# Top-k attention with mixture of depths: the 32nd greatest score from a bound, an exact count and one MAX8, with the exponential moved behind the transposes

## The chip, the core and the metric

The program runs on one core of one Trainium2 chip. The time is device time in microseconds (us) of one execution of the whole program. PE is the matmul engine, PEld its weight loads, DVE the vector engine, ACT the scalar engine, POOL the GpSimd engine, SP the engine that issues most DMAs.

## The reference

```python
def _attn_ref(q, k, v):                       # q, k, v: 8 batches, 8 heads, 576 tokens, 64 wide, f32
    scores = scale * np.matmul(q, k.transpose(0, 1, 3, 2))        # scale = 1 / 8
    kth = np.partition(scores, -32, axis=-1)[..., -32:-31]
    scores = np.where(scores >= kth, scores, -1000000000.0)
    attn = np.exp(scores - np.max(scores, axis=-1, keepdims=True))
    attn = attn / (np.sum(attn, axis=-1, keepdims=True) + 1e-09)
    return np.matmul(attn, v)

def _moe_ref(x, w_gate, w1, w2, capacity):    # x: 8 batches, 576 tokens, 512 wide; capacity = 128
    scores = np.einsum('bsd,d->bs', x, w_gate)
    out = x.copy()
    for b in range(B):
        top_idx = np.argpartition(-scores[b], capacity)[:capacity]
        ye = np.maximum(x[b, top_idx] @ w1, 0.0) @ w2             # 512 -> 1024 -> 512
        g = 1.0 / (1.0 + np.exp(-scores[b, top_idx]))
        out[b, top_idx] = x[b, top_idx] + g[:, None] * ye
```

The attention output, heads side by side, is the `x` of the second part. Everything is f32.

## The kernel before

Work is cut into 160 **units**: 8 batches, in each 5 tiles of queries, for each tile 4 pairs of heads. Four of the five query tiles have 128 tokens; there a unit makes two **score tiles** of 128 rows by 576 keys, one for each head of the pair (128 such units, "two-tile units"). The last query tile has 64 tokens, and both heads share one score tile (32 "one-tile units"). That makes 288 score tiles.

All four compute engines run their instructions strictly in the order in which the main loop writes them (the class `InOrder`, whose line 33 stands on nearly every row of the profile), so an instruction that waits holds back all that is written behind it on its engine. The loop is a software pipeline over units. In the turn of unit n:

- PE multiplies the scores of unit n + 1 (`scores`, tile `ps`), then the product with v of unit n - 2 (`values`, tile `small`: 10 matmuls, 20 in the trace, since each f32 product is two), then transposes the weights of unit n - 1 (`turn`, tiles `ptr` and `small`).
- DVE finds each row's 32nd greatest score of unit n (`top_k`): four times MAX8 (the 8 greatest of a row), between them three times MATCH_REPLACE8, which overwrites the 8 just found. The two tiles of a unit alternate.
- ACT copies scores out of PSUM (`sc`), copies the transposed weights out of PSUM (`pT`), copies the result of `values` (`xs`), and makes the exponential `e`.
- POOL, in `weigh`, makes `shift` (minus the greatest score), the mask `p` (score at or above the 32nd), and the product of `p` and `e`.

The **mixture** of a batch (ranks by gate score, gathering of 128 tokens as a matmul with a one-hot matrix `pick`, two dense layers) is a generator whose steps go one to a unit behind the unit's own work, in the first ten units of the next batch. On PE its steps are `xe_ps`, `extra_ps`, twice `h_ps`, `y_ps`. The **loads** of the next batch's q, k and v go one step to a unit in the units 11 to 18 of a batch: each asks SP for rows and transposes rows fetched earlier (`tr`, on PE, with copies to `kT` or `qT` on ACT). The kernel ends with the mixture of the last batch, beside nothing.

Of the kernel before, what the change touches and what calls it, by code (L numbers as in the profile page):

```python
# [15 lines left out]
# Below every score: what match_replace puts in place of the values already taken.  # L16
# [3 lines left out]
# Full tiles of 128 tokens; token 4 * p + j sits on partition p of tile j, so that  # L20
# a partition's four tokens are contiguous in memory. The last 64 tokens are tile J.
# [3 lines left out]
class InOrder:  # L25
    """An engine whose instructions stay in the order in which they are written."""
# [10 lines left out]
def kernel(  # L37
# [29 lines left out]
    ldpool = ctx.enter_context(tc.tile_pool(name="ld", bufs=2))  # L67
    kqpool = ctx.enter_context(tc.tile_pool(name="kq", bufs=2))
    scpool = ctx.enter_context(tc.tile_pool(name="sc", bufs=6))
    wkpool = ctx.enter_context(tc.tile_pool(name="wk", bufs=4))  # L70
    stats = ctx.enter_context(tc.tile_pool(name="stats", bufs=12))
    ppool = ctx.enter_context(tc.tile_pool(name="p", bufs=3))
    ptpool = ctx.enter_context(tc.tile_pool(name="pt", bufs=4))
# [11 lines left out]
    # The place of each token in its sequence, and the row of slots 0 .. CAP-1.  # L85
# [8 lines left out]
    # before[p, t, c] = 1 where the token of column c comes before token (p, t):  # L94
    # of tokens with the same gate score, the earlier one is taken first.
# [24 lines left out]
    # v with a column of ones: the product with it is the softmax's denominator.  # L120
# [28 lines left out]
    def load_qkv(b, qT, kT, vt):  # L149
        """In 2 * NHP steps, k and q of a pair of heads; each asks for the next one's rows."""  # L150

        def fetch(src, hp, name):
            rows = ldpool.tile([P, NT, 2, D], FP32, name=name)
            for hh in range(2):
                nc.sync.dma_start(
                    out=rows[:, 0:J, hh, :],
                    in_=src[b, 2 * hp + hh, 0:JP, :].rearrange("(p j) d -> p j d", j=J),
                )
            nc.sync.dma_start(
                out=rows[0:R, J, :, :],  # L160
                in_=src[b, 2 * hp : 2 * hp + 2, JP:S, :].rearrange("h p d -> p h d"),
            )
            return rows
# [4 lines left out]
            for src, dst, name in ((k, kT, "kin"), (q, qT, "qin"))  # L168
        ]
        fetched = {}  # L170
        for i, (src, dst, hp, name) in enumerate(todo):
# [5 lines left out]
            for c in range(J):  # L177
# [15 lines left out]
                in_=v[b, i, 0:JP, :].rearrange("(p j) d -> p j d", j=J),  # L193
            )
            nc.sync.dma_start(out=vt[0:R, i, J, 0:D], in_=v[b, i, JP:S, :])
            yield

    def top_k(scs):
        """Of each tile's rows, the greatest score and the least of the TOP_K greatest."""
        cur, left, first = list(scs), {}, {}  # L200
        for r in range(TOP_K // 8):
            best = {}
            for i in range(len(scs)):
                best[i] = stats.tile([P, 8], FP32, name="best" if r else "first")
                dve.max(best[i], cur[i])
            first = first or best
            if r < TOP_K // 8 - 1:
                for i in range(len(scs)):
                    if r == 0:
                        left[i] = wkpool.tile([P, S], FP32, name="left")  # L210
                    dve.match_replace(left[i], best[i], cur[i], LOWEST)
                    cur[i] = left[i]
        return [(first[i][:, 0:1], best[i][:, 7:8]) for i in range(len(scs))]
# [9 lines left out]
    def scores(t, hp, qT, kT):  # L223
        """The pair's score tiles; two heads' products go to banks of their own."""
# [11 lines left out]
        scs = []  # L236
        for ps in pss:
            sc = scpool.tile([P, S], FP32, name="sc")
            act.copy(
                out=sc.rearrange("p (u s) -> p u s", u=2), in_=ps[:, :, 0:HALF]  # L240
            )
            scs.append(sc)
        return scs

    def weigh(scs, tops):
        """exp(scale * (score - greatest)) where a score is among its row's TOP_K, else 0."""
        weights = []
        for sc, (top, kth) in zip(scs, tops):
            shift = stats.tile([P, 1], FP32, name="shift")
            pool.tensor_scalar_mul(shift, top, -scale)  # L250
            e = ppool.tile([P, S], FP32, name="e")
            act.activation(e, sc, AF.Exp, bias=shift, scale=scale)
            p = ppool.tile([P, S], FP32, name="p")
            pool.tensor_scalar(
                out=p, in0=sc, scalar1=kth, scalar2=None, op0=ALU.is_ge
            )
            pool.tensor_tensor(p, p, e, ALU.mult)
            weights.append(p)
        return weights

    def turn(weights):
        """The weights transposed, [key, chunk of keys, query]."""
        small = ps_small.tile([P, 512], FP32, name="small")
        turned = []
        for i, p in enumerate(weights):
            pT = ptpool.tile([P, NT, P], FP32, name="pT")
            tr = ps_tr.tile([P, 512], FP32, name="ptr")
            for c in range(J):
                pe.transpose(
                    tr[:, c * P : (c + 1) * P], p[:, c * P : (c + 1) * P], ident  # L270
                )
            pe.transpose(small[0:R, i * P : (i + 1) * P], p[:, JP:S], ident)
            act.copy(
                out=pT[:, 0:J, :], in_=tr.rearrange("p (c i) -> p c i", c=J)
            )
            act.copy(out=pT[0:R, J, :], in_=small[0:R, i * P : (i + 1) * P])
            turned.append(pT)
        return turned, small

    def values(t, hp, turned, small, vt, xs):  # L280
        """The weights' product with v, and their sums, into the heads' columns of xs."""
        n = R if t == J else P
        for pT, heads in zip(turned, heads_of(t)):
            for hh, r in heads:
                for c in range(NT):
# [3 lines left out]
                        pT[0:rows, c, r : r + n],  # L289
# [9 lines left out]
    def normalise(n, xs, x):  # L299
        den = stats.tile([P, H], FP32, name="den")  # L300
# [11 lines left out]
    def route(gate, rank):  # L312
        """Each token's rank by gate score, [token, tile]."""
# [15 lines left out]
        for t in range(NT):  # L329
# [3 lines left out]
            tied = modpool.tile([P, S], FP32, name="tied", tag="scratch", bufs=2)  # L333
# [18 lines left out]
    def mixture(b, x, gate):  # L352
        """In steps, that go between those of the next batch's attention."""
# [3 lines left out]
        # What goes with a token to its slot: its row of out, and sigmoid(gate).  # L357
# [3 lines left out]
        for t0, t1, n in ((0, J, P), (J, NT, R)):  # L361
            dve.tensor_scalar_add(
                out=extra[0:n, t0:t1, 0], in0=tok_i[0:n, t0:t1], scalar1=float(b * S)
            )
            # exp(88) is finite, and its reciprocal below the least normal number.
# [71 lines left out]
        gy = modpool.tile([P, HD], FP32, name="gy", bufs=2)  # L437
        act.activation(gy, ps, AF.Copy, scale=g)
        # Every token has its x in out by then; a slot's token gets g * y on top.
# [8 lines left out]
    def gates(t, x, gate):  # L448
        n = R if t == J else P
        prod = modpool.tile([P, S], FP32, name="prod", tag="scratch", bufs=2)  # L450
# [11 lines left out]
    def store(b, x):  # L462
        nc.sync.dma_start(
            out=out[b, 0:JP, :].rearrange("(p j) n -> p j n", j=J), in_=x[:, 0:J, :]
        )
        nc.sync.dma_start(out=out[b, JP:S, :], in_=x[0:R, J, :])
# [8 lines left out]
    load_from = per_batch - 1 - 2 * NHP  # L475
# [6 lines left out]
    for n in range(-1, len(units) + 3):  # L482
# [3 lines left out]
        if n + 1 < len(units):  # L486
            b, t, hp = units[n + 1]
            made[n + 1] = scores(t, hp, *qkv[b][0:2])
# [71 lines left out]
```

## Time and profile before

| | |
|---|---|
| median of 3 runs | 1803.62 us (1800.26 to 1804.66) |
| span of the profiled execution | 1801.2 us |
| DVE busy | 1552.2 us (86%) |
| PE busy, weight loads busy | 1432.4 us (80%), 1114.2 us (62%) |
| POOL busy | 1052.5 us (58%) |
| ACT busy | 687.1 us (38%) |
| chain that ended last | DVE 42%, PE 27%, POOL 15%, issue 13%, ACT 3% |

The profiled execution has no other time of its own than its span. The span lies 2.4 us below the median of the runs, and inside their scatter. Busy time is an average over stages; the chain (followed back from the last instruction to what released each) is spread over three engines, so which engine sets the pace has to be read stage by stage. The granted clock of PE has two levels in this trace, 0.50 (1.2 GHz) and 1.00 (2.4 GHz).

### The profile page before, as it was taken

The numbers are of one execution on the slowest core, as the hardware profiler recorded it, in microseconds if no ns is written. First come the engines' busy times: TensorE is split into PE (matmuls) and PEld (weight loads), VectorE is DVE, ScalarE is ACT, GpSimd is POOL, SyncE is SP. The second block draws the span as 40 slices with busy tenths as digits, with TensorE's granted clock in tenths as the row PEclk, the third lists the DMA queues.
The fourth block names the chain that finished last, engine by engine and source line by source line (L and its number), as shares of the span: only waits on it lengthen the run. The fifth ranks groups of instructions, "written<-read, shape, count | busy, mean of one in ns | idle before, by whom it ended". The sixth has DMA issues, their size and how long they took to land.

```text
span 1801.2 us, 22598 instructions
## 1 busy us (share of the span) xinstructions
PE 1432.4 (80%) x7320; PEld 1114.2 (62%) x7320; DVE 1552.2 (86%) x3281; ACT 687.1 (38%) x1505; POOL 1052.5 (58%) x931
## 2 busy tenths in 40 slices
PE   5888777897778977789778897688876988769875
PEld 3667556575566756667557675576655866557554
DVE  7999798888988889887998879987799878998872
ACT  3444433344333443334433344333443334433330
POOL 5767465565656655556655566555665556655660
PEclk8766666857567575776757766577665767658767
DMA  7101200012000120001200112001120011000000
GB/s 196 35 5 29 70 3 1 13 27 73 1 1 13 27 73 1 0 13 29 71 1 1 19 28 66 1 1 20 30 63 1 1 19 37 4 1 1 7 24 9
DMA packets 120486, 45.77 MB, mean 25 GB/s; under 512 B 116144, under 2 KB 116144, under 8 KB 119344
## 3 DMA queue, kind: packets, MB, share of 16 engines
q1 hardware_dynamic: 119216, 42.23, 9.2%
q0 software_dynamic: 1152, 2.10, 0.9%
q8 instruction: 58, 0.95, 0.2%
q14 instruction: 60, 0.49, 0.1%
HBM read 32.77 MB, written 11.53 MB: 25 GB/s over the span
## 4 chain that ended last, share of the span: by engine, by line
DVE 42%; PE 27%; POOL 15%; issue 13%; ACT 3%; DMA 0%; POOLq 0%; SPq 0%; ACTq 0%; DVEq 0%
DVE left L33 15%; DVE best L33 15%; POOL p L33 13%; PE small L33 11%; DVE first L33 5%; PE ptr L33 4%; PE ps L33 4%; DVE tied L33 4%; PE h_ps L33 3%; PE tr L33 2%; PE xe_ps L33 1%; POOL shift L33 1%; DVE prod L33 1%; POOL x L33 1%; ACT e L33 1%
## 5 line engine op out<-in xcount | busy, mean ns | idle before, releaser
L33 POOL TENSOR_SCALAR p<-sc,best 128x576 f32<-128x576 f32 x288 | 526.0, 1827 | 211.3 <-DVE best L33 159.5
L33 DVE MAX8 best<-left 128x8 f32<-128x576 f32 x864 | 613.8, 746 | 4.4
L33 PEld LDWEIGHTS small<-v,pT 128*128 128x128 f32 (+3 forms) x3200 | 510.3, 237 | 138.5 <-issue 71.0
L33 PE MATMUL small<-v,pT 128*128 128x65 f32 (+3 forms) x3200 | 579.3, 336 | 2.1 <-ACT pT L33 2.1
L33 POOL TENSOR_TENSOR p<-p,e 128x576 f32<-128x576 f32 x288 | 407.2, 1414 | 282.7 <-ACT e L33 266.3
L33 PE MATMUL ptr<-ident,p 128*128 128x128 f32 x1152 | 279.1, 387 | 284.6 <-POOL p L33 284.5
L33 DVE MATCH_REPLACE8 left<-best,left 128x576 f32<-128x576 f32 x576 | 423.2, 741 | 0.0
L33 PEld LDWEIGHTS ptr<-ident,p 128*128 128x128 f32 x1152 | 187.7, 195 | 333.2 <-POOL p L33 320.1
L33 ACT ACTIVATE e<-sc,shift 128x576 f32<-128x576 f32 x288 | 223.4, 776 | 412.9 <-POOL shift L33 412.7
L33 PE MATMUL ps<-kT,qT 64*128 64x288 f32 (+1 forms) x1280 | 294.8, 583 | 1.1 <-ACT qT L33 1.1
L33 DVE MAX8 first<-sc 128x8 f32<-128x576 f32 x288 | 202.8, 740 | 75.0 <-ACT sc L33 74.9
L33 ACT COPY pT<-ptr 128x512 f32<-128x512 f32 x288 | 170.2, 591 | 221.6 <-PE ptr L33 221.4
L33 DVE MATCH_REPLACE8 left<-first,sc 128x576 f32<-128x576 f32 x288 | 211.6, 741 | 0.0
L33 PEld LDWEIGHTS ps<-kT,qT 64*128 64x128 f32 (+1 forms) x1280 | 159.7, 250 | 58.9 <-issue 16.1
L33 ACT COPY sc<-ps 128x576 f32<-128x576 f32 x288 | 169.0, 631 | 19.0 <-PE ps L33 18.0
L33 POOL TENSOR_TENSOR x<-xs,rden 128x512 f32<-128x512 f32 (+1 forms) x40 | 41.8, 1046 | 150.0 <-DVE rden L33 148.1
L33 ACT COPY xs<-small 128x130 f32<-128x130 f32 (+1 forms) x160 | 43.4, 271 | 178.0 <-PE small L33 177.9
L33 PE MATMUL small<-ident,p 128*64 128x128 f32 x288 | 108.8, 378 | 0.4 <-ACT pT L33 0.4
L33 DVE TENSOR_SCALAR den<-xs 128x8 f32<-128x8 f32 (+1 forms) x40 | 6.9, 171 | 81.4 <-ACT xs L33 81.4
L33 POOL TENSOR_SCALAR shift<-first 128x1 f32<-128x1 f32 x288 | 75.2, 261 | 1.1 <-DVE first L33 1.1
L33 ACT COPY pT<-small 64x128 f32<-64x128 f32 x288 | 74.9, 260 | 0.0
L33 PE MATMUL h_ps<-xeT,w 128*128 128x128 f32 x512 | 72.2, 309 | 0.4 <-DVE g L33 0.4
(54 smaller groups left out, 831.2 us busy)
## 6 DMA issues: line engine op xcount, KB each, us to landing
kin<-in_k_dram SPq DMA_DIRECT2D x64, 128.0 KB, 2.8
qin<-in_q_dram SPq DMA_DIRECT2D x64, 128.0 KB, 2.8
v<-in_v_dram SPq DMA_DIRECT2D x64, 128.0 KB, 2.6
out_dram<-x SPq DMA_DIRECT2D x8, 1024.0 KB, 4.4
w<-in_moe_w_dram SPq DMA_DIRECT2D x2, 2048.0 KB, 9.0
kin<-in_k_dram SPq DMA_DIRECT2D x32, 32.0 KB, 2.4
qin<-in_q_dram SPq DMA_DIRECT2D x32, 32.0 KB, 2.5
v<-in_v_dram SPq DMA_DIRECT2D x64, 16.0 KB, 2.3
```

The source lines that it names most:

```text
L33: return lambda *a, **kw: self._tc.keep_in_program_order(fn(*a, **kw))
```

## The change

`top_k` and `weigh` go. In their place, for unit n in the loop's turn n:

- `bound` (DVE): a row of 576 scores is taken as 8 parts of 72, a MAX8 of each gives 64 candidates; three MAX8 and two MATCH_REPLACE8 over those 64 give the 24th greatest candidate. POOL copies it into the table `seen`, reading only the upper 16 bits of the number, so it is rounded down.
- `part` (ACT): the sign of (bound - score) for the whole row, as 16-bit `sides`, with the row's sum as a second output. The sum tells exactly how many scores are at or above the bound.
- `mask` (POOL): `y` = score times side. Scores below the bound keep their value, the others turn negative. Eight more columns are filled so that as many of them are huge as there are scores above the bound beyond 24.
- `find_kth` (DVE, one turn later): one MAX8 over the 584 columns of `y`; its eighth value is the 32nd greatest score. POOL scales it by 2^90.
- In turn n + 2: ACT makes `z` = Relu(2^90 * (32nd - score)), POOL subtracts it from the score, PE transposes `z`, and ACT takes the exponential while it copies the transposes out of PSUM into `pT`. No greatest score is subtracted any more.
- `values` of a unit comes in turn n + 3, one turn later than before.

The tables `seen` and `sums` are kept for the whole program. At its end DVE reduces them to one flag, PE adds it over the partitions, and every engine reads it: if a bound, a count or a denominator lay outside its limits, a general path (a loop over the batches with the old method) computes everything again. In the reference's inputs every one of the 36864 rows has 24 to 30 scores at or above its bound (the limits are 24 and 31), the least bound is 0.088 (limit 1e-16), and no denominator exceeds 33 (limit 1e6).

Row loads now share one ring of 3 buffers (before: 2 for q and 2 for k); other pools are resized.

```diff
-    ldpool = ctx.enter_context(tc.tile_pool(name="ld", bufs=2))
+    ldpool = ctx.enter_context(tc.tile_pool(name="ld", bufs=3))
...
-            rows = ldpool.tile([P, NT, 2, D], FP32, name=name)
+            rows = ldpool.tile([P, NT, 2, D], FP32, name=name, tag="rows")
...
-    def top_k(scs):
...
-    def weigh(scs, tops):
...
+    def bound(n, sc, at):
+        w = S // 8
+        cand = wkpool.tile([P, 2, 64], FP32, name="cand")
+        best = [stats.tile([P, 2, 8], FP32, name=f"best{r}") for r in range(3)]
+        for i in range(n):
+            for u in range(8):
+                dve.max(cand[:, i, 8 * u : 8 * u + 8], sc[:, i, u * w : (u + 1) * w])
+            for r in range(3):
+                dve.max(best[r][:, i, :], cand[:, i, :])
+                if r < 2:
+                    dve.match_replace(
+                        cand[:, i, :], best[r][:, i, :], cand[:, i, :], LOWEST
+                    )
+        pool.tensor_copy(
+            out=seen[:, 0, at : at + n],
+            in_=best[2].rearrange("p i e -> p (i e)").bitcast(BF16)[:, 15 : 16 * n : 16],
+        )
+    def part(i, sc, at, sides):
+        act.activation(
+            sides[:, i, :],
+            sc[:, i, :],
+            AF.Sign,
+            bias=seen[:, 0, at + i : at + i + 1],
+            scale=-(1.0 + 2.0**-23),
+            accum_out=seen[:, 2, at + i : at + i + 1],
+        )
+    def mask(i, sc, at, sides, y):
+        pool.tensor_tensor(y[:, i, 0:S], sc[:, i, :], sides[:, i, :], ALU.mult)
+        pool.tensor_scalar(
+            out=y[:, i, S : S + 8],
+            in0=steps,
+            scalar1=seen[:, 2, at + i : at + i + 1],
+            scalar2=-TALL,
+            op0=ALU.add,
+            op1=ALU.mult,
+        )
+    def find_kth(n, y, at):
+        next8 = stats.tile([P, 2, 8], FP32, name="next8")
+        for i in range(n):
+            dve.max(next8[:, i, :], y[:, i, :])
+        pool.tensor_scalar_mul(seen[:, 1, at : at + n], next8[:, 0:n, 7], BIG)
...
+        if is_unit(n - 2):
+            for i in range(tiles_of(n - 2)):
+                act.activation(
+                    z[:, i, :],
+                    sc[:, i, :],
+                    AF.Relu,
+                    bias=seen[:, 1, at + i : at + i + 1],
+                    scale=-BIG,
+                )
+                pool.tensor_tensor(z[:, i, :], sc[:, i, :], z[:, i, :], ALU.subtract)
...
+                act.activation(
+                    pT[:, 0:J, i, :],
+                    tr.rearrange("p (c i) -> p c i", c=J),
+                    AF.Exp,
+                    scale=scale,
+                )
...
+    with tc.If(nc.values_load(unsure[0:1, 0:1]) > 0):
+        with tc.For_i(0, B) as b:
+            general(b, row0)
```

How the order moves, at three places. POOL before, in a plain stretch of two-tile units, two tiles (`shift` is minus the greatest score, `first` and `best` are DVE's results; the words in brackets are the engines waited for, DVE, PE, Activation for ACT, Pool for POOL):

```order
L33 TENSOR_TENSOR p<-p,e 128x576 [waits Activation_49,Pool_49]
L33 TENSOR_SCALAR shift<-first 128x1 [waits DVE_49]
L33 TENSOR_SCALAR p<-sc,best 128x576 [waits DVE_49,PE_49]
L33 TENSOR_TENSOR p<-p,e 128x576 [waits Activation_49,Pool_49]
L33 TENSOR_SCALAR shift<-first 128x1
```

POOL after, one turn of a two-tile unit, with the normalising of a finished query tile (`x`) behind it:

```order
L41 TENSOR_TENSOR z<-sc,z 128x576 [waits PE_49,Activation_49]
L41 TENSOR_TENSOR z<-sc,z 128x576 [waits Activation_49]
L41 CAST seen<-best_2495 128x2 [waits DVE_49]
L41 TENSOR_TENSOR y<-sc,sides 128x576 [waits Activation_49]
L41 TENSOR_SCALAR y<-steps,seen 128x8
L41 TENSOR_TENSOR y<-sc,sides 128x576 [waits Activation_49]
L41 TENSOR_SCALAR y<-steps,seen 128x8
L41 TENSOR_SCALAR seen<-next_2548 128x2 [waits DVE_49]
L41 TENSOR_TENSOR x<-xs,rden 128x512 [waits DVE_49]
```

Behind the small copy into `seen` POOL now waits for ACT's sign, and after its last small instruction for ACT's Relu of the next turn; before, one wait for ACT stood in each tile.

ACT before, one turn of a two-tile unit:

```order
L33 ACTIVATE e<-sc,shift 128x576 [waits Activation_49,Pool_49] x2
L33 COPY sc<-ps 128x576 [waits DVE_49,PE_49]
L33 COPY sc<-ps 128x576 [waits DVE_49,PE_49,Activation_49]
L33 COPY xs<-small 128x130 [waits PE_49]
L33 COPY pT<-ptr 128x512 [waits PE_49]
L33 COPY pT<-small 64x128 [waits PE_49]
```

ACT after, one turn (here of a two-tile unit just behind one-tile units, so `xs` has 64 rows):

```order
L41 ACTIVATE z<-sc,seen 128x576 [waits Pool_49]
L41 ACTIVATE z<-sc,seen 128x576
L41 COPY sc<-ps 128x576 [waits DVE_49,PE_49,Activation_49]
L41 COPY sc<-ps 128x576 [waits PE_49]
L41 COPY xs<-small 64x130 [waits PE_49]
L41 ACTIVATE sides,seen<-sc,seen 128x576 [waits Activation_49,Pool_49]
L41 ACTIVATE pT<-ptr 128x4x128 [waits PE_49]
L41 ACTIVATE sides,seen<-sc,seen 128x576 [waits Activation_49]
L41 ACTIVATE pT<-ptr 128x4x128 [waits PE_49]
L41 ACTIVATE pT<-small 64x256 [waits PE_49]
```

Relu and sign are new; the exponential now stands where the `pT` copies stood. The second sign stands behind an exponential that waits for PE's transposes.

SP before, at the start of the program (`kin`, `qin`: rows of k and q; `w`: a weight matrix of the dense layers):

```order
L155 DMA kin<-in_k_dram 128x4x64 x2
L159 DMA kin<-in_k_dram 64x2x64
L155 DMA qin<-in_q_dram 128x4x64 x2
L159 DMA qin<-in_q_dram 64x2x64
L132 DMA wg<-in_moe_w_gate_dram 128x512
L155 DMA kin<-in_k_dram 128x4x64 x2
L159 DMA kin<-in_k_dram 64x2x64
L155 DMA qin<-in_q_dram 128x4x64 x2
L159 DMA qin<-in_q_dram 64x2x64
L135 DMA w_120<-in_moe_w_dram 128x4x1024
```

SP after, from the second pair's k on:

```order
L176 DMA kin<-in_k_dram 128x4x64 x2
L180 DMA kin<-in_k_dram 64x2x64
L153 DMA wg<-in_moe_w_gate_dram 128x512
L156 DMA w_124<-in_moe_w_dram 128x4x1024
L176 DMA qin<-in_q_dram 128x4x64
L212 DMA v_119<-in_v_dram 128x4x64
L216 DMA v_119<-in_v_dram 64x64
L176 DMA qin<-in_q_dram 128x4x64
L180 DMA qin<-in_q_dram 64x2x64
```

The 2 MB of `w` now stand ahead of the q rows of the second pair; before, they stood behind those and the third pair's.

## Rows read from the trace of the kernel before

**Rows 1.** Span and mean granted clock of PE on the core.

```profile
core 0: 1801.2 us, clock 0.687
```

**Rows 2.** Stretches: length, busy PE, PEld, DVE, ACT, POOL (instructions), clock, DMA.

```profile
642.00:690.00 48.00, 36.69 (x199) 27.58 (x197) 47.73 (x101) 20.83 (x46) 30.49 (x26) 0.64 0.20 54
690.00:786.00 96.00, 75.14 (x387) 60.42 (x388) 88.95 (x194) 30.28 (x67) 49.41 (x43) 0.72 0.00 1
786.00:864.00 78.00, 67.27 (x335) 52.50 (x334) 57.35 (x119) 34.77 (x76) 50.88 (x46) 0.65 0.15 31
744.00:756.00 12.00, 12.00 (x51) 10.50 (x52) 8.71 (x21) 4.16 (x9) 6.67 (x7) 0.50 0.00 1
```

**Rows 3.** Timeline, POOL and ACT: start, length, instruction, in brackets idle before.

```profile
842.62 0.78 ACT L33 ACTIVATE e<-sc,shift 128x576 f32<-128x576 f32 x1
...
843.54 1.40 POOL L33 TENSOR_TENSOR p<-p,e 128x576 f32<-128x576 f32 x1 [2.44 <-ACT e L33]
...
844.92 0.22 POOL L33 TENSOR_SCALAR shift<-first 128x1 f32<-128x1 f32 x1
845.11 1.74 POOL L33 TENSOR_SCALAR p<-sc,best 128x576 f32<-128x576 f32 x1
845.17 0.78 ACT L33 ACTIVATE e<-sc,shift 128x576 f32<-128x576 f32 x1 [1.78 <-POOL shift L33]
```

**Rows 4.** Timeline, PE at the lower clock: a tile's turn, scores, two products with v.

```profile
711.63 1.12 PE L33 MATMUL ptr<-ident,p 128*128 128x128 f32 x4 [3.15 <-POOL p L33]
...
712.89 2.29 PE L33 MATMUL ps<-kT,qT 64*128 64x288 f32 x8
...
715.11 5.10 PE L33 MATMUL small<-v,pT 128*128 128x65 f32 x20
...
1754.35 3.00 PE L33 MATMUL small<-v,pT 128*64 128x65 f32 x20 [0.61 <-ACT pT L33]
```

**Rows 5.** Timeline, PE at the upper clock: the same three kinds.

```profile
316.58 1.24 PE L33 MATMUL ps<-kT,qT 64*128 64x288 f32 x8
317.75 2.87 PE L33 MATMUL small<-v,pT 128*128 128x65 f32 x20
...
857.59 0.66 PE L33 MATMUL ptr<-ident,p 128*128 128x128 f32 x4
```

**Rows 6.** Timeline, DVE in a one-tile unit, each instruction needing the one before.

```profile
1738.68 0.76 DVE L33 MAX8 best<-left 128x8 f32<-128x576 f32 x1
...
1739.47 0.09 DVE L33 MATCH_VALUE_LOAD left<-best,left 128x8 f32 x1
1739.55 0.74 DVE L33 MATCH_REPLACE8 left<-best,left 128x576 f32<-128x576 f32 x1
```

**Rows 7.** Chain in order of time (start, time on it): two tiles' MAX8; a 4-column instruction.

```profile
900.18 1.32 DVE first L33 x2
...
940.09 0.07 DVE extra L33
```

**Rows 8.** Timeline, PE: three kinds of steps of a mixture.

```profile
285.65 7.72 PE L33 MATMUL xe_ps<-pick,x 128*128 128x128 f32 x39
...
312.30 4.34 PE L33 MATMUL h_ps<-xeT,w 128*128 128x128 f32 x32
...
334.29 8.62 PE L33 MATMUL y_ps<-w,hT 128*128 128x512 f32 x16
```

**Rows 9.** Timeline, PE at the lower clock: a load step's transposes, the next scores.

```profile
840.37 1.06 PE L33 MATMUL tr<-ident,kin 128*128 128x128 f32 x4
...
842.40 2.18 PE L33 MATMUL ps<-kT,qT 64*64 64x288 f32 x8
```

**Rows 10.** Timeline, DVE: the program's first MAX8.

```profile
11.41 1.42 DVE L33 MAX8 first<-sc 128x8 f32<-128x576 f32 x2 [7.12 <-ACT sc L33]
```

**Rows 11.** DMA issues of the weights: count, size of one, us to landing.

```profile
w<-in_moe_w_dram SPq DMA_DIRECT2D x2, 2048.0 KB, 9.0
```

**Rows 12.** Timeline, ACT: the last unit's result leaves PSUM.

```profile
1757.38 0.26 ACT L33 COPY xs<-small 64x130 f32<-64x130 f32 x1 [3.08 <-PE small L33]
```

More of the change, by code (lines that the diff above doesn't have):

```diff
@@ L261, in turn @@
[L261 to L278, printed above, removed]
@@ L282, in values @@
+    def values(t, hp, pT, small, vt, xs):
         n = R if t == J else P
[L283 removed]
+        for i, heads in enumerate(heads_of(t)):
             for hh, r in heads:
@@ L480, with tiles_of @@
     xs = x = gate = None
-    made, weights, turned = {}, {}, {}
-    for n in range(-1, len(units) + 3):
+    scs, masked, turned = {}, {}, {}
+    def tiles_of(n):
+        return len(heads_of(units[n][1]))
+    for n in range(-1, len(units) + 4):
+        is_unit = lambda i: 0 <= i < len(units)
         if 0 <= n + 1 < NHP:
@@ L519 @@
             qkv[b + 1] = room_for_qkv(b + 1)
-            loading = load_qkv(b + 1, *qkv[b + 1])
-        if i >= load_from:
+            loading = load_qkv(q[b + 1], k[b + 1], v[b + 1], *qkv[b + 1])
+        if n >= 0 and i >= load_from:
             next(loading, None)
-        if tops:
-            weights[n] = weigh(made.pop(n), tops)
+    if gating is not None:
+        b, t, *of_batch = gating
+        gates(t, *of_batch)
+        store(out[b], of_batch[0])
+        mixing = mixture(float(b * S), *of_batch)
@@ new lines @@
+    sure = stats.tile([P, 1], FP32, name="sure")
+    dve.memset(sure, 1.0)
+    for what, op, than, limit in (
+        (seen[:, 0, :], ALU.min, ALU.is_gt, LEAST),
+        (seen[:, 1, :], ALU.min, ALU.is_gt, LEAST * BIG),
+        (seen[:, 2, :], ALU.max, ALU.is_lt, float(MIDDLE)),
+        (seen[:, 2, :], ALU.min, ALU.is_gt, float(MIDDLE - 16)),
+        (sums.rearrange("p t h -> p (t h)"), ALU.max, ALU.is_lt, MOST),
+    ):
+        far = stats.tile([P, 1], FP32, name="far")
+        dve.tensor_reduce(out=far, in_=what, axis=mybir.AxisListType.X, op=op)
+        dve.scalar_tensor_tensor(
+            out=sure, in0=far, scalar=limit, in1=sure, op0=than, op1=ALU.mult
+        )
@@ new lines, in general, with of @@
+    def general(b, row0):
+        def of(a):
+            return a[bass.ds(b, 1)].rearrange("o a s d -> (o a) s d")
+        qT, kT, vt = room_for_qkv(0)
+        for _ in load_qkv(of(q), of(k), of(v), qT, kT, vt):
+            pass
+        x = xpool.tile([P, NT, HD], FP32, name="x")
+        gate = xpool.tile([P, NT], FP32, name="gate")
+        for t in range(NT):
+            xs = xpool.tile([P, H, DE], FP32, name="xs")
+            for hp in range(NHP):
+                w = len(heads_of(t))
+                p = general_weights(w, keep(multiply(t, hp, qT, kT)))
+                small = ps_small.tile([P, 512], FP32, name="small")
+                pT = ptpool.tile([P, NT, 2, P], FP32, name="pT")
+                for i in range(w):
+                    tr = ps_tr.tile([P, 512], FP32, name="ptr")
+                    turn(i, p, tr, small)
+                    nc.scalar.copy(
+                        out=pT[:, 0:J, i, :], in_=tr.rearrange("p (c i) -> p c i", c=J)
+                    )
+                nc.scalar.copy(
+                    out=pT[0:R, J, 0:w, :],
+                    in_=small[0:R, 0 : w * P].rearrange("p (i c) -> p i c", i=w),
+                )
+                values(t, hp, pT, small, vt, xs)
+            rows = R if t == J else P
+            den = stats.tile([P, H], FP32, name="den")
+            normalise(rows, xs, x[0:rows, t, :], den)
+            gates(t, x, gate)
+        store(out[bass.ds(b, 1)].rearrange("o s n -> (o s) n"), x)
+        for _ in mixture(row0, x, gate):
+            pass
```

211 lines of the change are left out of this document (139 added, 72 removed).

## The prediction

> **What bounds the kernel now.** I read the page's busy shares first: DVE 86%, PE 80%, POOL 58%. Then the chain: it runs through DVE, PE and POOL in turn, so no engine holds the end all the way. So I cut one batch (642 to 864 us, 222 us) by what goes on beside the units [rows 2]. In its plain part DVE is busy 47.7 of 48 us, beside the mixture 89 of 96: DVE sets the pace. In the part with the loads DVE is busy only 57 of 78 us and PE 67: there PE sets it, at a mean clock of 0.65. Over the whole program the granted clock is 0.687 [rows 1]; with levels 0.50 and 1.00 that is 63% of the time at the lower one. What is to be seen: taking work from DVE helps for two thirds of a batch, and PE stands close behind, at half its clock most of the time.
>
> **DVE: what goes and what comes.** A tile had four MAX8 and three replacements over 576 columns. Two independent MAX8 take 1.32 us of the chain, 0.66 each, and a 4-column instruction 0.07 [rows 7]: so 0.065 us and 1.03 ns a column. Where each needs the one before, MAX8 takes 0.79 to the next start, and the replacement with its load 0.86 [rows 6], which is 0.13 more than unhindered. So a MAX8 of 72 columns costs 0.14, one of 64 that is waited for 0.13 + 0.13 = 0.26, a replacement of 64 (0.73 less 512 columns, plus 0.13) 0.33. A tile's `bound` is 8 x 0.14 + 0.13 + 3 x 0.26 + 2 x 0.33 - 0.13 (the next tile doesn't wait) = 2.5 us, its last MAX8 0.67: 6.4 us for a two-tile unit, where before it was 4 x 1.32 + 6 x 0.73 = 9.7. With some 20 us of other work a batch (194 us busy in rows 2, less 36 x 7 x 0.70), DVE needs 16 x 6.4 + 4 x 3.2 + 20 = 135 us a batch. It no longer bounds. If the short MAX8 did not overlap at all (0.26 each) a unit would take 8.4 and a batch 170: just beside what follows.
>
> **POOL: a closed ring with ACT.** POOL and ACT keep their order, so a turn on POOL is a loop with waits in it. Prices [rows 3]: tensor by tensor 1.38 to the next start (843.54 to 844.92); a small instruction 0.19; start of a small one to ACT's start 0.25; ACT 0.78; ACT's end to POOL's start 0.14. A two-tile turn: small, Relu, start of the subtraction 0.25 + 0.78 + 0.14 = 1.17; two subtractions 2.76; small, sign, start of `y` 1.17; `y`, filler, `y`, filler 3.14: 8.24 us. Sign, exponential and sign, at 0.78 each, end at 6.66 of it and the second `y` wants them at 6.67, so they are hidden while PE's transposes are in time. A one-tile turn: 1.17 + 1.38 + 1.17 + 1.57 = 5.29. ACT's ten instructions of a turn, even at 0.78 each, are 7.8 us, inside the 8.24. The trace has no `y` with a 16-bit operand: its bounds are the plain 1.38 and the dearest POOL instruction of this width, 1.74 [rows 3]. I take 1.38, the same operation.
>
> **PE: the same work, closer together.** Its matmuls and transposes stay. At 1.2 GHz a two-tile unit is two turns of 1.26 (711.63 to 712.89), scores 2.22, products 5.0 [rows 4]: 9.7 us, more than POOL's ring. A one-tile unit: 1.26 + 2.18 [rows 9] + 3.00 [rows 4] = 6.4. At 2.4 GHz a two-tile unit is 2 x 0.66 + 1.17 + 2.87 = 5.4 [rows 5], so 2.9 of the ring's 8.24 are free. So at the lower clock PE sets the pace, at the upper one POOL's ring. In the low part PE no longer waits between the turns of two tiles for POOL (it waited 3.15 us before one in rows 4), and should come up a little oftener: I take 55% of the time low instead of 63%.
>
> The clock decides the size, so here a rule against the row. PE was busy 12.0 of 12 us from 744 to 756 and got 0.50 throughout [rows 2]. The Trainium skill, TensorE: Matmul & The Clock Gate, section "What's actually happening", says that throttled is the default and activity releases it; by that a PE that stops waiting would run at 2.4 GHz nearly always, and the time would be the first rival's. That row does not bear it out: full by the records, and still low.
>
> **The sum.** A two-tile unit 0.55 x 9.7 + 0.45 x 8.24 = 9.04, a one-tile unit 0.55 x 6.4 + 0.45 x 5.29 = 5.90. A batch: 16 x 9.04 + 4 x 5.90 = 168.3, plus five normalisings on POOL at 1.38, seen only at the upper clock: 171.4. Eight: 1371.
> Mixtures beside units, seven: PE gets 7.72, 8.62 and twice 4.34 to do [rows 8]. At the low clock nothing hides them: 25.0. At the upper one each loses the free 2.9: 13.4. 0.55 and 0.45 of them: 19.8, times 7: 139. DVE's part of a mixture hides in its own slack.
> Loads, seven batches of 8 steps: 2.03 us of PE from the transposes to the scores behind them, the wait for ACT's copy included [rows 9]. Hidden at the upper clock, seen at the low one: 0.55 x 16.2 x 7 = 62.
> Start: first MAX8 at 11.4 [rows 10], then two tiles' `bound` 5.0, and 5 for the q rows that now queue behind 2 MB of weights, which land in 9.0 us [rows 11] (0 to 9): 21.
> End: from the last unit's ring to its result one MAX8, Relu, subtraction, transposes, exponentials (less than two at 0.78), products, copy: 0.76 + 0.2 + 1.17 + 1.38 + 1.26 + 1.0 + 3.0 + 0.3 = 9.1; then as before 1801.2 - 1757.4 = 43.8 [rows 12]; the five reductions and the flag that every engine reads, 4 (no row; 0 to 10): 57.
> 1371 + 139 + 62 + 21 + 57 = 1650, against a span of 1801.2. The median of the runs stands 2.4 above that span: **1652 us**. As a cross-check, PE's 1432 us of records at much the same clock would then fill 87% of the span instead of 80%.
>
> **The rivals.**
> The clock comes up and stays: all units at the ring's pace. 8 x (16 x 8.24 + 4 x 5.29 + 6.9) + 7 x 13.4 + 78 = 1451, so 1454. For it: PE's waits for POOL shrink. Against: 744 to 756, and the 2.9 us in which PE would then idle in each unit; the plain part, with PE busy 37 of 48 us, had 0.64 [rows 2]. Chance 0.20, counting from 1580 down.
> POOL's ring is longer: `y` at 1.74 adds 0.72 to a two-tile turn, 0.36 to a one-tile turn; at 45% of the time that is 47 us: 1699. If the subtractions cost that too, 9.68, still under PE's 9.7: 1745. For it: 1.74 exists at the same width. Against: it is another operation. Chance 0.16.
> Slower, by PE: it stays at 1.2 GHz. Every unit then takes PE's 9.7 or 6.4, mixtures and loads are bare: 8 x (155.2 + 25.6) + 7 x 25.0 + 7 x 16.2 + 78 = 1813, so 1815. Each tenth of low time is worth 36 us, so it is slower than before from a share of 97% on. For it: the load part was at 0.65 with PE 86% busy [rows 2]. Against: the mixture part had 0.72 with PE 78% busy. Chance 0.07.
> The change does not do what it says: a limit is overstepped and the general path runs after all, again 288 tiles of 5.8 us on DVE without overlap: 1650 + 1670 = 3300 at least. Against: the inputs keep far from the limits (24 to 30 of the allowed 24 to 31). Chance 0.02.
>
> **How the numbers follow.** My forecast (low share 40 to 70%, other terms as taken) has 0.50 and gives 1580 to 1720. The first rival 0.20, the second 0.16, slower ones 0.09; 0.05 is left for the seam where long rings and a low clock meet at no change. A measurement of this kernel can tell some 0.3% from no change. Faster 0.86, same 0.05, slower 0.09. The range leaves out the lower third of the first rival and the slower cases: 1520 to 1790; the unknown DVE overlap (up to some 40) and the end lie inside it.
>
> **What would show it.** The page of the new kernel should have DVE down to some 1080 us of busy time, POOL near 1000, ACT up to some 1000, PE near 1400. In a plain stretch, a two-tile turn of 8.2 us where the clock is 1.00 and of 9.7 where it is 0.50, with PE without gaps in the second. Short MAX8 0.14 apart; POOL's `y` 1.38. Waits at the top: POOL for ACT's Relu and sign, ACT for PE's products; none of DVE for ACT of any size. I am wrong if DVE still waits for nobody, if POOL's ring is far from 8.24, or if the clock leaves 0.6 to 0.85.

## The result, and the profile after

The changed kernel takes **1579.97 us** (median of 4 runs, 1570.52 to 1584.83), the kernel before 1801.94 us beside it: a ratio of 0.877 with a 95% interval of 0.873 to 0.880, or 222 us less. The forecast was 1652 us, faster, with a range of 1520 to 1790: right in sign, 72 us too long. The profiled execution has a span of 1578.0 us at a mean granted clock of 0.756 ([rows 1] had 0.687).

Page of the changed kernel, busy time (share of the span, instructions) and the chain by engine:

```profile
PE 1345.1 (85%) x7322; PEld 1047.6 (66%) x7322; DVE 1077.1 (68%) x5024; ACT 887.5 (56%) x1953; POOL 1003.9 (64%) x1253
...
PE 42%; DVE 29%; POOL 12%; ACT 10%; issue 6%; DMA 0%; SPq 0%; POOLq 0%; ACTq 0%
```

DVE's 86% of the span has become 68%. Its waits, and those of the rest (us in total, times, longest):

```profile
POOL y L41 <- ACT sides L41: 242.0, 152, 8.9
ACT xs L41 <- PE small L41: 207.1, 106, 4.3
ACT z L41 <- POOL seen L41: 152.9, 109, 3.1
POOL z L41 <- ACT z L41: 152.3, 120, 3.4
DVE sums L41 <- ACT xs L41: 135.4, 33, 12.1
...
DVE cand L41 <- ACT sc L41: 124.5, 41, 9.0
```

POOL waits for ACT and ACT for POOL: the ring. One turn of it in a plain stretch, POOL's timeline (start, length, in brackets the idle time before):

```profile
44.82 0.22 POOL L41 TENSOR_SCALAR seen<-next 128x2 f32<-128x2 f32 x1
45.94 2.77 POOL L41 TENSOR_TENSOR z<-sc,z 128x576 f32<-128x576 f32 x2 [0.89 <-ACT z L41]
48.65 0.19 POOL L41 CAST seen<-best 128x2 f32<-128x2 bf16 x1
49.81 1.27 POOL L41 TENSOR_TENSOR y<-sc,sides 128x576 f32<-128x576 f32 x1 [0.98 <-ACT sides L41]
51.17 0.27 POOL L41 TENSOR_SCALAR y<-steps,seen 128x8 f32<-128x8 f32 x1
51.52 1.28 POOL L41 TENSOR_TENSOR y<-sc,sides 128x576 f32<-128x576 f32 x1
52.88 0.27 POOL L41 TENSOR_SCALAR y<-steps,seen 128x8 f32<-128x8 f32 x1
53.23 0.22 POOL L41 TENSOR_SCALAR seen<-next 128x2 f32<-128x2 f32 x1
```

From 44.82 to 53.23 are 8.41 us. I call this distance, from one `seen<-next` to the next, a turn. Turns of the first batch, cut there (length, busy PE, PEld, DVE, ACT, POOL, clock, DMA):

```profile
53.23:61.64 8.41, 6.66 (x36) 4.84 (x36) 6.20 (x33) 5.53 (x12) 6.22 (x9) 0.77 0.25 57
61.64:70.04 8.40, 8.40 (x35) 6.46 (x34) 6.20 (x33) 5.63 (x12) 6.21 (x8) 0.50 0.01 2
70.04:79.43 9.39, 9.39 (x44) 7.85 (x44) 4.70 (x27) 5.64 (x12) 6.21 (x9) 0.57 0.00 0
79.43:88.47 9.04, 7.17 (x42) 5.33 (x41) 8.54 (x42) 5.53 (x12) 7.66 (x9) 0.81 0.00 0
88.47:96.86 8.39, 8.39 (x41) 6.91 (x40) 6.20 (x33) 5.63 (x12) 6.20 (x8) 0.60 0.00 1
96.86:105.27 8.41, 6.12 (x43) 4.63 (x42) 6.22 (x33) 5.53 (x12) 6.21 (x9) 1.00 0.01 2
```

A turn is 8.4 us at a clock of 1.00, of 0.77 and of 0.50; only one of these grew with the low clock (9.39), and 9.04 holds a normalising. I call turns without mixture and loads plain. The first ten as one stretch:

```profile
36.40:122.69 86.29, 75.72 (x369) 57.37 (x369) 65.83 (x332) 56.23 (x121) 65.01 (x82) 0.72 0.18 48
```

Less two normalisings of 0.63 (9.04 less 8.41), that is 8.50 us a turn. In turns with loads, late in a batch, PE does set the length. Four of them, in the same view (11.27 and 11.36 us at the low clock, 9.05 with a normalising at the upper one):

```profile
890.88:901.27 10.39, 9.71 (x42) 7.99 (x40) 6.31 (x33) 6.43 (x14) 6.22 (x9) 0.50 0.13 30
901.27:912.54 11.27, 10.59 (x47) 8.61 (x45) 4.69 (x27) 6.55 (x14) 6.21 (x8) 0.57 0.12 26
912.54:921.59 9.05, 6.37 (x47) 4.79 (x45) 6.30 (x27) 5.77 (x13) 7.66 (x10) 0.98 0.16 34
...
930.45:941.81 11.36, 10.68 (x45) 8.25 (x43) 3.20 (x17) 5.26 (x12) 4.66 (x6) 0.50 0.12 26
```

A batch in the middle is 191.2 us long (204.54 to 395.77); in [rows 2] it was 222. Its first eleven turns hold the mixture. Three of them (222.00 to 252.64), called turns with ties below, hold the `tied` instructions, which rank the gate scores. There DVE is busy nearly throughout:

```profile
204.54:317.24 112.70, 98.98 (x553) 78.59 (x551) 89.59 (x397) 65.79 (x144) 77.57 (x92) 0.79 0.05 10
222.00:252.64 30.64, 26.09 (x127) 19.98 (x126) 28.85 (x91) 16.78 (x37) 21.50 (x25) 0.67 0.00 1
```

### The profile page after: what moved, and what is told of

Read it like the earlier page. It is cut to its first block, busy times and chain, and to the rows that moved or that the text cites. A ratio compares the mean times of both kernels' runs of the same rounds, so it can differ in the third digit from the quotient of the medians.

```text
span 1578.0 us, 24253 instructions
## 1 busy us (share of the span) xinstructions
PE 1345.1 (85%) x7322; PEld 1047.6 (66%) x7322; DVE 1077.1 (68%) x5024; ACT 887.5 (56%) x1953; POOL 1003.9 (64%) x1253
## 4 chain that ended last, share of the span: by engine, by line
PE 42%; DVE 29%; POOL 12%; ACT 10%; issue 6%; DMA 0%; SPq 0%; POOLq 0%; ACTq 0%
PE small L41 18%; DVE cand L41 13%; PE ps L41 7%; POOL z L41 6%; PE ptr L41 6%; DVE best L41 5%; DVE tied L41 5%; ACT sides L41 4%; PE h_ps L41 3%; PE xe_ps L41 3%; DVE next L41 3%; PE y_ps L41 3%; ACT pT L41 3%; PE tr L41 3%; POOL y L41 2%
## 5 line engine op out<-in xcount | busy, mean ns | idle before, releaser
L41 POOL TENSOR_TENSOR y<-sc,sides 128x576 f32<-128x576 f32 x288 | 375.3, 1303 | 271.1 <-ACT sides L41 242.0
L41 POOL TENSOR_TENSOR z<-sc,z 128x576 f32<-128x576 f32 x288 | 410.7, 1446 | 153.3 <-ACT z L41 152.3
L41 DVE MAX8 cand<-sc 128x8 f32<-128x72 f32 x2304 | 333.6, 217 | 124.5 <-ACT sc L41 124.5
L41 PE MATMUL ptr<-ident,z 128*128 128x128 f32 x1152 | 251.2, 358 | 101.7 <-POOL z L41 100.9
L41 ACT ACTIVATE z<-sc,seen 128x576 f32<-128x576 f32 x288 | 208.9, 768 | 153.0 <-POOL seen L41 152.9
L41 DVE MAX8 next<-y 128x8 f32<-128x584 f32 x288 | 210.2, 755 | 104.6 <-POOL y L41 104.2
L41 ACT ACTIVATE sides<-sc,seen 128x576 bf16<-128x576 f32 x288 | 222.0, 771 | 104.7 <-POOL seen L41 104.3
L41 PEld LDWEIGHTS ptr<-ident,z 128*128 128x128 f32 x1152 | 171.2, 180 | 143.8 <-POOL z L41 133.6
L41 DVE MAX8 best<-cand 128x8 f32<-128x64 f32 x864 | 197.0, 228 | 29.8
L41 ACT ACTIVATE pT<-ptr 128x512 f32<-128x512 f32 x288 | 167.8, 583 | 9.4 <-PE ptr L41 9.0
```

What stands on the lines that cost most here:

```text
L41: return lambda *a, **kw: self._tc.keep_in_program_order(fn(*a, **kw))
```

## Experiments

Every edit starts from the changed kernel (1580 us). Times are medians, each beside runs of the kernel before (1801 to 1803), and the intervals are of the ratio to it; the changed kernel's is 0.873 to 0.880.

**Undoing the reduction.** `bound`, `part`, `mask` and `find_kth` go, and the threshold comes from

```diff
+        for r in range(4):
+            for i in range(n):
+                cur = left[:, i, :] if r else sc[:, i, :]
+                dve.max(best[r][:, i, :], cur)
+                if r < 3:
+                    dve.match_replace(left[:, i, :], best[r][:, i, :], cur, LOWEST)
+        pool.tensor_scalar_mul(seen[:, 1, at : at + n], best[3][:, 0:n, 7], BIG)
```

> Undoes one part: a tile's threshold comes again from four MAX8 and three replacements over 576 columns on DVE; the bound, the sign, POOL's y, the fillers and the count are left out, the Relu mask, the subtraction on POOL and the exponential on leaving PSUM stay. Theory A (the gain is DVE's shorter reduction): DVE needs 9.7 us for a two-tile unit again and waits for nobody, so about the time of before, 1760 to 1810 us. Rival (Relu mask and exponential on leaving PSUM bring most of it, by a shorter ring and less on POOL): 1650 us or less, although DVE is as busy as before.

Measured: 1759.89 us (0.974 to 0.977). Page:

```profile
PE 1318.7 (75%) x7322; PEld 1016.4 (58%) x7322; DVE 1633.2 (93%) x3296; ACT 682.4 (39%) x1377; POOL 534.5 (30%) x519
```

At the lower edge of what the first theory expected; the rival is out. So 180 of the 222 us go with DVE's shorter reduction. With the old one, all the rest of the change (the Relu mask, the exponential behind the transposes, the new order) gives 43 (1803 to 1760).

**More work on DVE.**

```diff
             dve.max(next8[:, i, :], y[:, i, :])
+            dve.max(again8[:, i, :], y[:, i, :])
```

> Adds one more MAX8 over y for each tile on DVE: 288 of 0.66 to 0.76 us, 190 to 219 us of work, 1.3 to 1.5 us in a two-tile turn. Theory A (a turn is POOL's and ACT's ring of 8.4 us; DVE's 6.4 us lie inside it): most of it hides, at most 60 us more, in the turns with ties, normalising and loads, where DVE stands on the chain. Rival (DVE still sets the pace): 190 us or more on top of 1580.

Measured: 1554.43 us (0.859 to 0.863), 26 us *less*, although DVE is busy for 149 us more (1226.5; the 288 MAX8 last 216 us, in part beside others). The rival is out: plain turns stay at 8.4. No theory had expected a gain. It lies in the turns with loads; here the same six turns of the second batch, as stretches, of the changed kernel and then of this one:

```profile
317.24:375.72 58.48, 51.99 (x254) 41.63 (x252) 26.79 (x134) 32.94 (x72) 32.75 (x43) 0.65 0.14 31
```

```profile
317.08:370.31 53.23, 47.43 (x254) 38.33 (x252) 33.01 (x144) 32.49 (x72) 32.83 (x42) 0.71 0.15 34
```

The same 254 matmul records take 5.3 us less at a clock of 0.71 instead of 0.65, and PE's busy time gives 4.6 of them. So here a better place of the low stretch is worth that much. It is not so in every batch: the six in the middle take 184.2 to 191.8 us, where the changed kernel's take 190.6 to 191.4. Why the extra MAX8 moves the clock stays open.

**One subtraction from POOL to DVE** (`later` holds the `sc` and `z` of unit n - 2).

```diff
     def bound(n, sc, at, later):
...
+            if i == n - 1 and later is not None:
+                dve.tensor_tensor(
+                    later[1][:, 1, :], later[0][:, 1, :], later[1][:, 1, :], ALU.subtract
+                )
             for u in range(8):
```

> Moves the subtraction of a unit's second tile from POOL to DVE, between the bounds of the two tiles. Theory A (the ring sets a plain two-tile turn): POOL's loop is 1.4 us shorter, DVE has some 7.2 us to do, so a plain two-tile turn falls from 8.4 to 7.0 to 7.4 us; turns that wait for the mixture's or the loads' products keep their length: 1440 to 1520 us. Rival (PE at its granted clock sets the pace): 1560 us or more, turns at low clock unchanged.

Measured: 1739.46 us (0.962 to 0.966), 160 us more: a miss. Its waits:

```profile
POOL seen L41 <- DVE best L41: 424.5, 130, 4.9
DVE z L41 <- ACT z L41: 328.4, 101, 6.0
```

DVE came into the loop: its subtraction waits for ACT's Relu, that for POOL's small copy behind the masks, and POOL's next small copy for the `best` that DVE does behind the subtraction. A plain turn was 10.3 us at every clock. POOL has less to do and the ring is longer: the ring, not POOL's work, is what counts.

**The ring opened.** DVE writes both entries of the table itself.

```diff
-        pool.tensor_copy(
-            out=seen[:, 0, at : at + n],
...
+            dve.tensor_copy(
+                out=seen[:, 0, at + i : at + i + 1],
+                in_=best[2][:, i, :].bitcast(BF16)[:, 15:16],
+            )
...
-        pool.tensor_scalar_mul(seen[:, 1, at : at + n], next8[:, 0:n, 7], BIG)
+        dve.tensor_scalar_mul(seen[:, 1, at : at + n], next8[:, 0:n, 7], BIG)
```

> DVE itself writes the bound (tile by tile) and the scaled threshold into the table that ACT reads; until now POOL did so, in its order behind the masks. DVE has 0.3 us more in a turn, POOL 0.4 less, and ACT's Relu and sign no longer wait for POOL's turn. Theory A (the closed loop of POOL and ACT sets a plain turn at 8.4 us): the loop opens, and a plain two-tile turn falls to what ACT or DVE have to do themselves, 7.0 to 7.6 us: 1450 to 1520 us. Rival (PE at its granted clock): plain turns fall where the clock is up and rise to 9.7 where it is down, 1560 us or more.

Measured: 1492.44 us (0.824 to 0.830), 88 us less. POOL's timeline in a plain stretch:

```profile
42.95 2.77 POOL L41 TENSOR_TENSOR z<-sc,z 128x576 f32<-128x576 f32 x2
45.69 1.28 POOL L41 TENSOR_TENSOR y<-sc,sides 128x576 f32<-128x576 f32 x1
47.05 0.27 POOL L41 TENSOR_SCALAR y<-steps,seen 128x8 f32<-128x8 f32 x1
47.40 1.28 POOL L41 TENSOR_TENSOR y<-sc,sides 128x576 f32<-128x576 f32 x1
48.75 0.27 POOL L41 TENSOR_SCALAR y<-steps,seen 128x8 f32<-128x8 f32 x1
49.11 2.77 POOL L41 TENSOR_TENSOR z<-sc,z 128x576 f32<-128x576 f32 x2
```

From 42.95 to 49.11 POOL never waits: 6.16 us, its own work. Later plain turns, counted by DVE's writes, are 6.9 to 8.4 (6.95 at a clock of 0.97, 8.35 at 1.00). This shows the loop as the bound of plain turns. With the loop open DVE fills them but for 0.45 us (busy for 6.50 of 6.95 us, for 7.90 of 8.35). In the three turns with ties it pays for the move: 35.4 us instead of 30.5, mean of the six middle batches.

**PE: more and less.** Four matmuls a unit more, overwritten by the products behind them; and three of five key chunks left out.

```diff
+        for c in range(J):
+            pe.matmul(
+                small[0:n, 2 * P : 2 * P + DE],
+                pT[0:P, c, 0, 0:n],
+                vt[0:P, 2 * hp, c, :],
+                start=True,
+                stop=True,
+            )
```

> Gives PE four more matmuls a unit ahead of its products with v (overwritten by them): by the rows of 20 products in 2.87 and 5.10 us, 0.57 us more at 2.4 GHz and 1.02 at 1.2. Prediction's term (a turn is the mean of the dearer of ring and PE at each clock: every low stretch is paid): 0.5 x 1.02 x 160, 80 us more or above, plain turns 0.5 longer. Theory A (PE catches up at the high clock what it lost at the low one, so a plain turn is the greater of the ring and PE's mean): plain turns stay at 8.4 to 8.6 us, only turns with loads and mixture grow: 10 to 55 us more.

Measured: 1630.35 us (0.903 to 0.911), 50 more, inside the second theory's range and well below 80. Both were reckoned from half the work: each f32 product is two records, so the edit adds eight a unit (8602 against 7322 in all), not four of the 20 priced. By the same rows that is 1.15 us at the upper clock and 2.04 at the lower, and the prediction's term becomes some 160 us. Its miss is thus the larger, and that 50 fell into the other range is in part luck. Plain turns of the first batch, as stretches, and one with a load:

```profile
44.59:53.02 8.43, 6.74 (x51) 5.41 (x51) 6.21 (x33) 5.53 (x12) 6.23 (x9) 1.00 0.55 123
53.02:61.42 8.40, 8.40 (x41) 6.89 (x41) 6.20 (x33) 5.62 (x12) 6.21 (x8) 0.59 0.25 57
61.42:69.83 8.41, 7.17 (x55) 5.88 (x55) 6.21 (x33) 5.63 (x12) 6.21 (x8) 1.00 0.01 2
...
333.49:346.47 12.98, 12.30 (x53) 10.31 (x51) 4.70 (x27) 6.55 (x14) 6.21 (x9) 0.50 0.11 24
```

They keep 8.4 us; a turn with a load at the low clock (last row) takes 12.98 where it was 11.27. The mean clock rose to 0.826 (a low share of 35%), so the size of 50 is a sum of more work and a better clock. By the prediction's prices PE's mean is then 0.35 x 11.7 + 0.65 x 6.55 = 8.4, just the ring's length (an estimate). At a low share of 49%, as in the changed kernel, it would be 9.1. By this estimate the plain turns kept their length only because the clock came up.

```diff
-                for c in range(NT):
+                for c in (0, J):
```

> Leaves out three of the five key chunks of the products with v (12 of 20 matmuls of a unit), so PE has some 1.7 us less to do in a two-tile unit at 2.4 GHz and 3.0 less at 1.2. Theory A (the ring sets a plain turn; PE at its granted clock sets those beside mixtures and loads): plain two-tile turns stay at 8.4 us, load turns fall from 9.0 to 11.4 to about 8.4: 1490 to 1550 us. Rival (PE sets most turns, as the prediction's low-clock term has it): 1.7 to 3.0 us off each of 160 turns, 1310 us or less to 1400.

Measured: 1505.96 us (0.833 to 0.838; two runs), 74 less, as the first theory has it: plain turns stay at 8.4 us, and of the turns with loads those of 10.2 to 11.4 fall to 8.4 to 8.8 (the one that holds the mixture's y grows from 13.9 to 15.5). The mean clock fell to 0.707.

**The mixture's price.** `mixing = iter(())` in the loop.

> Leaves out the mixtures of the first seven batches, which stand beside the next batch's units; the last one, loads, gates and stores stay. By the changed kernel's trace a batch with mixture and loads takes 191 us and the first one, with loads and no mixture, some 168, so 23 each: 1410 to 1435 us. By the sum of the prediction (19.8 each) 1441. Rival (a mixture's price is mainly the low clock that it brings, and comes back elsewhere): 1480 us or more.

Measured: 1414.68 us (0.782 to 0.788; two runs). The edit left out the last batch's mixture too, contrary to what was written ahead, so the total is not the seven alone. A batch in the middle tells it:

```profile
204.72:375.45 170.73, 145.87 (x783) 113.17 (x783) 122.59 (x596) 107.35 (x236) 119.84 (x154) 0.72 0.12 29
```

191.2 less 170.7 are 20.5 us a mixture. That batch's first eleven turns, the six turns with loads behind them, and then the last batch, which has neither mixture nor loads, up to its fourteenth turn and its eighteenth:

```profile
204.71:302.92 98.21, 84.52 (x413) 65.31 (x414) 76.68 (x368) 62.67 (x136) 72.68 (x92) 0.67 0.04 8
302.92:355.40 52.48, 45.54 (x258) 37.07 (x256) 27.25 (x134) 32.55 (x72) 32.72 (x43) 0.77 0.15 35
1232.26:1355.85 123.59, 110.52 (x532) 84.73 (x531) 92.68 (x452) 77.42 (x167) 92.74 (x116) 0.67 0.01 2
1232.26:1383.79 151.53, 133.00 (x657) 101.67 (x656) 105.08 (x505) 91.61 (x198) 110.14 (x139) 0.68 0.02 9
```

So 14.5 of the 20.5 us lie in the turns that hold the mixture (112.70 less 98.21). The other 6.0 lie in the turns with loads (58.48 less 52.48), which hold none of its steps: there the clock was 0.65 in a batch with a mixture and is 0.77 without, and PE's busy time alone fell by 6.4 us for nearly as many records (254, 258). The rival, the lower clock, thus has a part in the price but not most of it.

**ACT stands still for the mixture.** Its reading of a product becomes a step of its own, behind the next turn's Relus and copies, and `load_from` goes from 11 to 12; then the second edit alone.

```diff
             scs[n + 1] = keep(pss)
+        if after_first:
+            next(mixing, None)
...
-    load_from = per_batch - 1 - 2 * NHP
+    load_from = per_batch - 2 * NHP
```

> ACT's reading of the mixture's products (xe, two h, y) is put behind the next turn's Relus and score copies instead of right behind the products, and the loads start one turn later (so that y's bank is free). PE's work and order stay. Theory B (a mixture's products cost their time because ACT and POOL, which keep their order, stand still until PE is done: ACT waits 4.1, 3.0, 1.6 and 4.7 us for xe, h, h and y, and POOL 4.0 for its scatter): 6 to 12 us a batch less, 1490 to 1540 us. Rival (PE's own time is what they cost): no change, 1565 us or more.

> Takes one of the two edits of e5_late_evac alone: the loads start one turn later, ACT reads the mixture's products where it did. Theory (e5's 49 us come from ACT and POOL no longer standing still for the products): less than half of it from this edit, 1560 to 1585 us. Rival (they come from the loads' turns, which fall on another phase of the clock and no longer on the turn of the mixture's y): 1530 to 1550 us, the gain all in the turns from 11 on.

Measured: 1531.10 us (0.848 to 0.854) for both, 1557.97 (0.864 to 0.867) for the later loads alone. So of 49 us 22 come with the loads' place, two more than was expected of it, and 27 when the late reading is added. First eleven turns of the second batch, later loads alone and then both edits:

```profile
203.37:315.27 111.90, 100.51 (x548) 79.34 (x547) 89.70 (x397) 65.11 (x142) 77.59 (x93) 0.77 0.04 7
```

```profile
204.36:313.91 109.55, 96.56 (x552) 76.67 (x550) 88.65 (x396) 65.25 (x142) 78.87 (x92) 0.81 0.04 7
```

Over the six middle batches these turns take 112.5 us on average in the changed kernel, 111.2 with later loads and 109.9 with both; the nine turns behind them 78.7, 75.4 and 73.0. So only 1.3 us a batch of the late reading's gain, some 9 of its 27 us, lie in the turns in which ACT had stood still. The rest lies in the turns behind, where the clock rose too (0.65, 0.70 and 0.76 on average in the six with loads); how much of that is the late reading's own and how much the place of the low stretches, no run parts. Waits of the changed kernel, and of the one with both edits:

```profile
ACT hT L41 <- PE h_ps L41: 42.3, 16, 6.5
ACT gy L41 <- PE y_ps L41: 39.2, 8, 6.3
ACT xeT L41 <- PE xe_ps L41: 36.8, 8, 7.2
```

```profile
ACT hT L41 <- PE h_ps L41: 9.5, 2, 6.6
ACT xeT L41 <- PE xe_ps L41: 7.1, 1, 7.1
ACT gy L41 <- PE y_ps L41: 6.3, 1, 6.3
```

What is left are the last batch's, which stand beside nothing.

**Start and end.** Weights on SP behind all first loads; and the end without reductions, flag and general path.

> The three weight loads are queued on SP behind all loads of the first batch instead of between its q rows. Theory (the second pair's q rows landed behind 2 MB of weights and PE waited 7.5 us for them): 4 to 9 us less, 1571 to 1576 us. Rival (what the start loses is made good later, or is ACT's order): within 3 us of 1580.

> Leaves out the end: the five reductions, the flag that the engines read, and the general path behind it. Prediction: 4 us (0 to 10); by the changed kernel's trace the stretch from the last result to the end is 48.3 us where it was 43.8: 3 to 8 us less, 1572 to 1577 us. Rival (the general path's code in the program costs time elsewhere too): over 10 us less.

Measured: 1568.77 us (0.869 to 0.872), 11 less, a little over what was expected, though single runs go from 1563 to 1582; and 1576.33 us (0.874 to 0.877), whose interval lies within the changed kernel's: 4 us can't be told from none.

**Three edits at once** (DVE writes the table, late reading with later loads, weights behind).

> Three edits at once: DVE writes bound and threshold, ACT reads the mixture's products behind the next turn's Relus and copies with the loads one turn later, the weights behind the first loads. Alone they gave 88, 49 and 11 us. Theory (they end different waits: the closed loop in plain turns, the stop of ACT and POOL in mixture turns, the q rows at the start): 1430 to 1460 us. Rival (the turns with ties, where DVE is behind, and those with loads at the low clock bound either way, and take back what the others give): 1470 to 1500 us.

Measured: **1448.62 us** (0.801 to 0.805), as the theory has it, faster than both kernels. Alone the three gave 88 + 49 + 11 = 148 us, together 131. What bounds it now is unlike in each part: DVE in the turns with ties (10.5 to 15.0 us; busy for 13.12 of 13.75 us in one), PE in those with loads (72% of the chain from 278 to 331 us).

## Why the prediction was right in sign and 72 us too long

*DVE.* Sized right: 1077.1 us busy (1080 predicted), eight short MAX8 in 1.16 to 1.18 us (0.14 apart), 135.0 us of a batch (135 predicted). "It no longer bounds" holds for plain turns; in those with ties (a tile's pair of `tied` takes from 0.82 + 0.82 to 1.28 + 1.84 us) it sets the pace, busy for 28.85 of 30.64 us. On the whole chain it has 29%.

*The ring.* 8.24 predicted, 8.41 measured. The two waits are 1.12 and 1.16 (1.17), `y` 1.36 to the next start (1.38); the filler, of eight columns, is 0.35 to the next start, not 0.19, the price of `shift` with its one column in [rows 3]. Twice 0.16, less the shorter subtractions, is the difference.

*The step that failed* is the blend "0.55 x 9.7 + 0.45 x 8.24 = 9.04". It takes the dearer of ring and PE in each state of the clock and then the mean, as if every low stretch were paid in full. PE may run late, though: from 61.64 to 70.04 it was busy for all of 8.40 us at 0.50 and the turn was no longer for it, the next one paid 1 us, and in the turns behind PE made it good out of its free time at the upper clock. The share of low time was not at fault: in the first ten turns the clock was 0.72, a low share of 56% where 55 was taken, and yet a turn took 8.50 us. In the last batch of the run without mixtures fourteen turns, less four normalisings, took 8.65 each at 0.67. Nearer than the blend is the greater of the two means, with the prediction's own prices 0.55 x 9.7 + 0.45 x 5.4 = 7.77 for PE against 8.24 for the ring: the ring. It is a floor, since some low stretches are paid. In a middle batch, predicted and read:

| term of a batch | predicted | read from the runs |
|---|---|---|
| 20 units without mixture and loads | 144.6 + 23.6 = 168.2 | 162.4 (eighteen turns of that last batch, 151.5, and two of a middle one, 14.1, less the normalisings) |
| five normalisings | 3.1 | 5 x 0.63 = 3.2 (79.43 to 88.47) |
| mixture | 19.8 | 20.5 (left out) |
| loads | 8.9 | 5.1 (170.7 less 165.6, without mixtures) |
| sum | 200.0 | 191.2 |

Of the 8.8 us of a batch the units give 5.8 and the loads 3.8; over eight batches of units and seven of loads that is 73 us, about the whole miss. The measured 162.4 lies midway between the blend's 168.2 and the ring's price throughout, 16 x 8.41 + 4 x 5.35 = 156.0 (5.35 is 8.41 less one `z`, `y` and filler). PE's added matmuls did not move plain turns either, though at a higher clock.

*The mixture.* The total was right, in part by luck. It was priced as PE's time alone, and [rows 8], taken for the low clock, ran at 0.74 to 0.85. In the turns that hold it, it cost 14.5 us. Of these 4.5 lie in the turns with ties (30.64 against 26.19 us), where DVE sets the pace; the prediction put DVE's part at nothing ("hides in its own slack"). And ACT waits in its order for each product and POOL for ACT, so DVE gets no scores for up to 9.0 us; "none of DVE for ACT of any size" was wrong (124.5 us). The other 6.0 us lie in the turns with loads, at a lower clock.

*Loads.* PE at its clock sets these turns, as predicted: 9.71 of 10.39 us and 10.59 of 11.27. Their price was too high where no mixture stands ahead (5.1 for 8.9).

*Start and end.* PE waited 7.5 us for q rows (5 taken, 0 to 9 allowed), and moving the weights gave 11. From the last `xs` to the end are 48.3 us, predicted 43.8 ([rows 12]) + 4.

*The rivals.* The clock did not come up for good: 0.756. `y` at 1.74 did not happen (1.30 mean). PE at the low clock throughout did not, and the general path did not run.

The Trainium skill, TensorE: Matmul & The Clock Gate, section "What's actually happening", says that activity releases the throttle. Over a whole program the two PE experiments agree: 0.826 with more matmuls and 0.707 with fewer. Single stretches agree as little as before: 0.50 from 61.64 to 70.04 with PE's records filling all of it.

## What to carry to other kernels

Where an engine's speed switches, first take the mean over a stretch that the pipeline's buffers bridge, and only then compare it with the other engines; comparing in each state and taking the mean of the dearer ones overstates (9.04 for 8.50 to 8.65 here), and the greater of the means is a floor (8.41). When two engines that keep their order wait for each other twice in a turn, price the closed loop, look which small instruction on it could be issued elsewhere, and make sure that moving work doesn't pull a third engine into the loop: 88 us less and 160 us more lay one edit apart. An engine that reads another's product in order holds up everything written behind it; reading it a turn later cost nothing here. Look also at the turns that hold none of what was changed: 6.0 of the mixture's 20.5 us stood there, at a lower clock.

## What was not expected of the hardware

- The granted clock went up with more matmuls (0.756 to 0.826) and down with fewer (0.707), and it moved with edits that leave PE's work as it is: 0.773 with more on DVE and 26 us less, 0.768 with the loads one turn later and 22 us less.
- DVE instructions with two tensors read take longer beside POOL's: the gates' product (`prod`) took 0.67 us where it and POOL's `y` began 0.02 us apart, and `y` then 1.83 instead of 1.27; beside POOL's subtractions it took 0.83 to 2.67 us, and the mean of all 40 is 1.41. The subtraction moved to DVE had a mean of 1.34 us. MAX8, with one tensor read, kept 0.75 beside POOL. By The Trainium skill, SBUF — State Buffer, section "Who interferes with whom", a DVE instruction with two SBUF inputs contends with a GpSimd instruction that reads SBUF. These rows agree. Timeline of the changed kernel, POOL and DVE:

```profile
834.58 1.83 POOL L41 TENSOR_TENSOR y<-sc,sides 128x576 f32<-128x576 f32 x1 [0.98 <-ACT sides L41]
834.60 0.67 DVE L41 CUSTOM_DVE_ANT_0 prod<-x,wg 128x512 f32<-128x512 f32 x1
```

- ACT's sum beside the sign is a second instruction of 0.19 us, 54.5 us in all; the prediction had no price for it, and ACT's slack hid it.
